# The opening's hand-written order changed by a few places in many entries, values loaded first, and late stores halved in place of late loads, in a fused linear-attention and PReLU-MLP kernel

## The chip, the cores and the metric

One core of one Trainium2 chip. The metric is the device time of one execution in microseconds (us); lower is better. The kernel before takes 220.07 us, the median of 3 runs (220.03 to 220.22).

## What is computed

Block-wise linear attention with a decay per head, and an MLP with a PReLU between its two matrices. q, k, v are (4 batches, 8 heads, 768 positions, 64), float32.

```python
for b in range(nb):                       # blocks of 64 positions
    intra = einsum('bhic,bhjc->bhij', qb, kb) * Dmask      # lam ** (i - j), causal
    intra = einsum('bhij,bhjd->bhid', intra, vb)
    inter = einsum('bhid,bhde->bhie', qb * lam_pow, kv_state)
    out[:, :, sl] = intra + inter
    kv_state = lam_block * kv_state + einsum('bhsd,bhse->bhde', kb * rev_pow, vb)
x = out.transpose(0, 2, 1, 3).reshape(3072, 512)
h = x @ w_in                              # 512 -> 2048
g = maximum(h, 0) + alpha * minimum(h, 0)
result = g @ w_out                        # 2048 -> 512
```

## The kernel before

**Tiling.** The 3072 positions are cut into 6 chunks c of 512: a third of the sequence (256 positions) of two batches. A chunk has four attention units, numbered n = 4c to 4c + 3: two batches (bi), two halves of the heads (hh, four heads each). On the kernel's own block size of 128 positions a unit has two blocks (a = 0, 1). The first four units, 0 to 3, are chunk 0; units 4 to 7 chunk 1, and so on.

**One unit.** `cast` (L267) copies its queries and keys to fp16; `turn` (L287) transposes them on TensorE, eight 128x128 transposes into the PSUM bank "tk", keys first, and `turned` (L300) copies the bank to qkT; from unit 8 on `turn_by_dma` (L305) does both as a DMA. `key_decayed` (L277) and `decayed` (L314) multiply keys and transposed queries by their decays. `cluster(old, new)` (L329) is TensorE's part: the scores s of the unit new, the output of the unit old from its masked scores sm and its states RD, and the state update kv of new, into the tile acc (or, with other=True, into banks 0 and 1, named h_acc). `masked` (L401) multiplies scores by the decay mask on VectorE. `state` (L418) makes the next state R from kv, on ScalarE where the state before is zero and on VectorE elsewhere; `spread` (L438) copies a state into the block-diagonal RD; `out_of` (L406) copies the unit's output to xT.

**The MLP.** `up(c, f, bi, slot)` (L453) makes 128 of the 2048 hidden features for a chunk, or for one batch of it (bi 0 or 1), in the PSUM bank slot; `below` (L466) is ScalarE's relu(-h), `gate` (L471) VectorE's combination of the two. `down` (L485) multiplies back, in four parts of four matmuls; `store` (L499) copies the result to SBUF on ScalarE and sends it out on ScalarE's DMA queue; `down_last` (L507) does both for the last chunk.

**Decays.** They depend on lam alone: `logs` takes logarithms, and `decay_mask`, `key_decay`, `query_decay`, `state_decay` (L201 to L224) exponentiate, all on ScalarE; `causal` (L206) clears the upper triangle of the masks on VectorE; `slopes` (L230) transposes alpha on TensorE into bank 0 and makes oma = 1 - alpha from it on VectorE.

**Loads.** `load` (L87) brings queries or keys as float32 on the SP queue, whole (512 KB) or a half of the heads (256 KB); `load16` (L100) brings queries or values as fp16 on POOL's queue, `load_win` and `load_wout` the weights likewise, a quarter each. `hold(x, c, bi)` (L83) writes one element of the tile that a load will fill, on VectorE: the load can't start before VectorE has reached that place in its order.

**The order.** The kernel turns the scheduler off. From L524 to the loop at L1097 each operation of the first three chunks is an entry in a list written out by hand; the engines run the entries in that order, each engine its own, and semaphores do the rest. A fixed PSUM bank is named by its slot. `fill(n, slot)` (L237) puts n matmuls of 128x128 on TensorE that nobody reads, into the bank of a slot (3 is the bank of the transposes). The loop from L1097 weaves the attention of the next chunk into the MLP of chunks 3 to 5, and loads two chunks ahead.

## Time and profile before

| | |
|---|---|
| median of 3 runs | 220.07 us |
| the profiled execution | 220.73 us |
| its span, first to last instruction | 218.6 us |
| TensorE (PE) busy | 207.1 us, 95% |
| VectorE (DVE) busy | 132.0 us, 60% |
| ScalarE (ACT) busy | 114.3 us, 52% |
| GpSimd (POOL) busy | 92.9 us, 43% |
| matmuls of fill | 132 of 2181 |
| mean granted TensorE clock | 0.999 |

The profile is of one execution. Times are from the first instruction of the span. A busy engine is one with an instruction in flight; TensorE's matmuls overlap, so that its busy time says that it was never idle, not that it ran at its peak. PEld is the weight load of TensorE, which overlaps with the matmuls; SP is the engine that only issues DMAs. A row of the timeline has the start in us, the length in us, engine, line, operation, what it writes and reads, the count, and in brackets how long the engine had been idle before it and what ended that. A row of the chain of waits has start, length and what the end of the kernel waited for then. A row of stretches has the window and its length, then for PE, PEld, DVE, ACT and POOL the busy time and the number of instructions, then clock, DMA share and GB/s. A row of DMA issues has what is loaded, the queue, the count, the size of one and the median us from issue to landing.

### The profile page before, as it was taken

Reading aid. Unit: us, or ns where it says so; the run is one execution under the profiler, and the core shown is the slowest. Engines: PE = TensorE matmul, PEld = TensorE weight load, DVE = VectorE, ACT = ScalarE, POOL = GpSimd, SP = SyncE. Lnnn points to the kernel's source line nnn. Section 1 sums busy time; section 2 is a strip of 40 time slices with the busy share of each in tenths; the row PEclk is TensorE's granted clock in tenths of the full one; section 3 lists DMA queues with packets and bytes.
Section 4 is the critical chain, followed back from the end, with each engine's and each line's share of the span. In section 5 each row is a group of like instructions: output and inputs, shape, how many; then the busy total and the mean of one; then the engine's idle time right before and its main releaser. Section 6 shows DMA issues by size and latency. Waiting matters only on the chain.

```text
span 218.6 us, 5366 instructions
## 1 busy us (share of the span) xinstructions
PE 207.1 (95%) x2181; PEld 112.5 (51%) x2181; DVE 132.0 (60%) x271; ACT 114.3 (52%) x225; POOL 92.9 (43%) x154
## 2 busy tenths in 40 slices
PE   4689799999999999999999999999999999999994
PEld 4577555564554554545445545554545444444442
DVE  2899488974688748778985646646645444444000
ACT  2996688741747534474746446445445444444120
POOL 8759996372546550736575374265231000000000
PEclk9999999999999999999999999999999999999999
DMA  3999999999999996499999441342211011110212
GB/s 105 231 190 221 191 212 219 214 210 204 312 229 197 305 212 209 60 143 163 250 236 121 97 96 33 66 96 59 40 51 48 1 51 48 48 45 3 99 48 97
DMA packets 62520, 29.85 MB, mean 137 GB/s; under 512 B 34192, under 2 KB 59552, under 8 KB 62496
## 3 DMA queue, kind: packets, MB, share of 16 engines
q1 hardware_dynamic: 38496, 15.01, 33.6%
q0 software_dynamic: 20368, 8.26, 30.6%
q10 hardware_dynamic: 3632, 6.24, 8.0%
q8 instruction: 17, 0.28, 0.5%
q14 instruction: 7, 0.06, 0.1%
HBM read 27.28 MB, written 6.29 MB: 154 GB/s over the span
## 4 chain that ended last, share of the span: by engine, by line
PE 78%; DMA 7%; ACT 6%; DVE 6%; issue 1%; ACTq 0%; DVEq 0%
PE h_ps L458 34%; PE o_ps L491 29%; PE o_ps L512 6%; DMA kraw<-in_k_dram 3%; PE s L363 3%; DMA qkT<-qk 2%; PE acc L375 2%; DMA lam_sb<-in_lam_dram 2%; PE acc L345 2%; DVE g L481 2%; ACT dmask L204 1%; ACT m L469 1%; DVE sm L404 1%; PE acc L392 1%; PE tp L294 1%
## 5 line engine op out<-in xcount | busy, mean ns | idle before, releaser
L481 DVE SCALAR_TENSOR_TENSOR g<-m,oma,h_ps 128x512 f16<-128x512 f32 (+1 forms) x104 | 72.0, 704 | 54.0 <-ACT m L469 53.6
L458 PE MATMUL h_ps<-xT,w_in_sb 128*128 128x512 f16 (+1 forms) x416 | 96.5, 363 | 0.5 <-DVE g L481 0.2
L469 ACT ACTIVATE m<-h_ps 128x512 f32<-128x512 f32 (+1 forms) x104 | 57.7, 563 | 60.0 <-PE h_ps L458 56.8
L491 PE MATMUL o_ps<-w_out_sb,g 128*128 128x512 f16 x320 | 79.9, 379 | 0.0
L458 PEld LDWEIGHTS <-w_in_sb 128*128 128x128 f16 x416 | 39.4, 98 | 42.6 <-issue 2.6
L491 PEld LDWEIGHTS <-g 128*128 128x128 f16 x320 | 30.5, 98 | 34.9
L255 POOL COPY RD<-R 64x128 f16<-64x128 f16 x54 | 16.2, 300 | 56.6 <-DVE R L429 54.7
L404 DVE TENSOR_TENSOR sm<-s,dmask 128x512 f16<-128x512 f32 x48 | 31.8, 683 | 3.3 <-PE s L363 3.2
L251 ACT ACTIVATE o_sb<-o_ps 128x512 f32<-128x512 f32 (+1 forms) x24 | 14.2, 592 | 22.4 <-PE o_ps L491 11.8
L282 POOL TENSOR_TENSOR kdec<-kraw,kdecay 128x512 f16<-128x512 f32 x21 | 22.2, 1061 | 1.9 <-DMA kraw<-in_k_dram 1.6
L319 POOL TENSOR_TENSOR qdT<-qkT,qdecay 128x512 f16<-128x512 f16 (+1 forms) x20 | 20.0, 1002 | 3.9 <-DMA qkT<-qk 3.1
L429 DVE SCALAR_TENSOR_TENSOR R<-R,rdecay,acc 128x64 f16<-128x64 f16 x60 | 13.9, 273 | 4.0 <-ACT xT L251 4.0
L251 ACT ACTIVATE xT<-acc 128x512 f16<-128x512 f32 x20 | 11.9, 596 | 7.9 <-PE acc L392 3.4
L241 PE MATMUL op_fill<-ident 128*128 128x128 f16 x132 | 10.5, 243 | 4.4 <-POOL ident masks.py:199 2.8
L512 PE MATMUL o_ps<-w_out_sb,g 128*128 128x512 f16 (+2 forms) x80 | 14.0, 336 | 0.0
L363 PE MATMUL s<-qkT 64*64 64x128 f16 x384 | 10.7, 222 | 1.4 <-DVE sm L404 0.8
L102 POOL DMA_DIRECT2D vh<-in_v_dram x13 | 11.7, 904 | 0.0
L241 PEld LDWEIGHTS <-ident 128*128 128x128 f16 x132 | 9.3, 111 | 4.6 <-POOL ident masks.py:199 2.8
L255 POOL CAST qk<-kraw 128x512 f16<-128x512 f32 x13 | 7.8, 610 | 8.1 <-DVE g L481 3.4
L512 PEld LDWEIGHTS <-g 128*128 128x128 f16 x80 | 7.2, 98 | 7.0
L363 PEld LDWEIGHTS <-qkT 64*64 64x64 f16 x384 | 6.5, 106 | 4.9 <-issue 1.4
L375 PE MATMUL acc<-sm,vh 64*64 64x128 f16 x352 | 8.8, 217 | 0.1
(69 smaller groups left out, 120.5 us busy)
## 6 DMA issues: line engine op xcount, KB each, us to landing
out_dram<-o_sb ACTq DMA_DIRECT2D x23, 256.0 KB, 2.2
kraw<-in_k_dram SPq DMA_DIRECT2D x12, 256.0 KB, 5.6
kraw<-in_k_dram SPq DMA_DIRECT2D x6, 512.0 KB, 8.3
qraw<-in_q_dram SPq DMA_DIRECT2D x6, 512.0 KB, 6.6
vh<-in_v_dram POOLq DMA_DIRECT2D x11, 256.0 KB, 6.8
w_in_sb<-in_moe_w_in_dram POOLq DMA_DIRECT2D x4, 512.0 KB, 8.9
w_out_sb<-in_moe_w_out_dram POOLq DMA_DIRECT2D x4, 512.0 KB, 15.4
qraw<-in_q_dram SPq DMA_DIRECT2D x5, 256.0 KB, 7.1
```

Source lines behind the costliest of these rows:

```text
L241: nc.tensor.matmul(t[:, 0:128], lhsT=ident, rhs=ident, start=True, stop=True)
L251: nc.scalar.activation(out, in_, AF.Copy)
L255: nc.gpsimd.tensor_copy(out=out, in_=in_)
L282: engine(eng).tensor_tensor(out=kdec, in0=kr, in1=d.unsqueeze(3).to_broadcast([128, 2, 4, D]), op=ALU.mult)
L319: engine(eng).tensor_tensor(out=qdT[:, :, :, p], in0=t["qkT"][:, 0, :, :, p], in1=qdecay[:, hh, :, :, p], op=ALU.mult,)
L363: nc.tensor.matmul(s[hl][ds(a * 64, 64), hp, 1 - e, :].rearrange("p (e j) -> p e j", e=2), lhsT=t["qkT"][p, 1, e, hp, ds(a * 64, 64)], rhs ...
L404: nc.vector.tensor_tensor(out=t["sm"][hl], in0=t["s"][hl], in1=mask_of(hl, units[n][2]), op=ALU.mult)
L458: nc.tensor.matmul(h_ps[:, 0:n] if bi is None else h_ps[:, 0:n].rearrange("p (e j) -> p e j", e=2), lhsT=w_in_sb[:, gi, ts(f, 128)], rhs=x ...
L469: nc.scalar.activation(m[:, 0:n], HP[c, f, bi][:, 0:n], AF.Relu, scale=-1.0)
L481: nc.vector.scalar_tensor_tensor(out=g, in0=mv, scalar=oma[:, f : f + 1], in1=hv, op0=ALU.mult, op1=ALU.add)
L491: nc.tensor.matmul(O[c, t], lhsT=G[c, f][:, t // 2, t % 2, :], rhs=w_out_sb[:, f, :], start=(f == 0), stop=(f == NF - 1),)
L512: nc.tensor.matmul(o_ps[:, 0:n], lhsT=G[c, f][:, t // 2, t % 2, :], rhs=w_out_sb[:, f, ds(c0, n)], start=(f == 0), stop=(f == NF - 1),)
```

## The change

- The list of the opening: nearly every entry up to turn(4) moves by a few places, many of the later ones by one or two. The first value load, load16("v", 0, 0, 1), becomes the first entry, ahead of the positions, and load16("v", 0, 0, 0) comes before identity. hold("k", 0, 1, 0) goes behind distances. slopes goes behind turn(1), turn(2) behind cluster(0, 1). hold("k", 1, 0) goes behind state(0, 1), hold("k", 1, 1) behind two gates. query_decay(3, 0) goes ahead of cast(4, "k").
- Engines: spread(0, 1), spread(4, 1), spread(9, 1) to ScalarE; cast(3, "q"), decayed(2), key_decayed(4), key_decayed(10), key_decayed(12), spread(11, 0) to VectorE; key_decayed(1) to POOL; spread(6, 1) stays there, two places later.
- fill: 165 matmuls in place of 132, in other places and banks.
- load("k", 4, bi) whole, the second half of the chunk first, in place of four halves; in the loop, for chunk 5, whole loads of keys and queries in place of halves.
- store: the results of chunk 4 and of the first two tiles of chunk 5 go out as two DMAs of 128x256 each in place of one of 128x512.

TensorE's order behind the opening is the same but for one place (up(1, 3, 1) goes behind down(1, 2, 2)).

```diff
@@ -501,8 +501,12 @@
         o_sb = o_pool.tile([128, DM], fp32, tag="osb", name="o_sb")
         copy_on("V" if last else "A", o_sb[:, 0:n], o_ps[:, 0:n])
         pb, b = c // 2, 2 * (c % 2) + t % 2
-        rows = out[ds(b * S + pb * W, W), ds(c0, n)].rearrange("(j e) d -> e j d", e=2)[t // 2]
-        (nc.sync if last else nc.scalar).dma_start(out=rows, in_=o_sb[:, 0:n])
+        w = n // 2 if (c, t) in HALVED else n
+        for x in range(0, n, w):
+            rows = out[ds(b * S + pb * W, W), ds(c0 + x, w)].rearrange("(j e) d -> e j d", e=2)[t // 2]
+            (nc.sync if last else nc.scalar).dma_start(out=rows, in_=o_sb[:, ds(x, w)])
+
+    HALVED = [(NC - 2, t) for t in range(4)] + [(NC - 1, t) for t in range(2)]
 
     def down_last(c, t, pieces):
         c0 = 0
@@ -521,132 +525,136 @@
 
 
 
+    load16("v", 0, 0, 1)
     positions()
-    warm_up()
-    load("q", 0, 0, 0)
-    identity()
-    load("k", 0, 0, 0)
-    hold("k", 0, 1, 0)
     load16("v", 0, 0, 0)
     distances()
+    load("q", 0, 0, 0)
+    warm_up()
+    hold("k", 0, 1, 0)
+    identity()
+    logs()
     load16("q", 0, 0, 1)
-    logs()
-    decay_mask(0)
+    load("k", 0, 0, 0)
+    cast(0, "k", "G")
+    load("k", 0, 1, 0)
+    query_decay(0, 0)
+    fill(38, 3)
     cast(0, "q", "A")
     key_decay()
-    query_decay(0, 0)
     decay_mask(1)
-    load16("v", 0, 0, 1)
-    cast(0, "k", "G")
     load_alpha()
-    fill(36, 2)
     turn(0)
+    load16("q", 0, 1)
     zeros()
     key_decayed(0, "V")
-    load16("q", 0, 1)
+    fill(6, 0)
     turned(0, "V")
+    decay_mask(0)
+    load_win(0)
+    load("k", 0, 0, 1)
+    fill(15, 2)
+    load16("v", 0, 1)
+    cluster(None, 0)
     decay_mask(3)
-    load("k", 0, 0, 1)
-    load16("v", 0, 1)
-    load_win(0)
+    query_decay(1, 1)
+    hold("k", 2, 0)
+    load16("v", 1, 0)
+    state(0, 0)
+    fill(6, 3)
     state_decay()
     decay_mask(2)
-    query_decay(1, 1)
-    fill(15, 2)
-    cluster(None, 0)
     causal(0)
-    load("k", 0, 1, 0)
-    state(0, 0)
-    hold("k", 2, 0)
+    spread(0, 1, "A", True)
+    fill(17)
+    cast(1, "k", "V")
+    fill(4, 2)
     cast(1, "q", "A")
-    cast(1, "k", "V")
-    fill(17)
-    spread(0, 1, "V", True)
-    load16("v", 1, 0)
     query_decay(0, 1)
+    turn(1)
     slopes(0)
-    fill(5, 2)
-    turn(1)
+    fill(5, 1)
+    key_decayed(1, "G")
+    load("k", 0, 1, 1)
+    query_decay(2, 1)
+    masked(0, 0)
     causal(1)
+    query_decay(3, 1)
+    fill(26, 2)
+    fill(14, 2)
+    masked(0, 1)
     cast(2, "q", "G")
-    masked(0, 0)
-    key_decayed(1, "V")
+    turned(1, "A")
+    cast(2, "k", "A")
     decayed(0, "G")
-    query_decay(3, 1)
-    turned(1, "A")
-    load("k", 0, 1, 1)
-    cast(2, "k", "A")
+    state(0, 1)
+    load16("q", 1, 0)
+    decayed(1, "G")
+    cluster(0, 1, True)
+    spread(1, 1, "A", True)
     hold("k", 1, 0)
-    masked(0, 1)
-    fill(26, 2)
+    cast(3, "k", "A")
     turn(2)
-    cluster(0, 1, True)
-    query_decay(2, 1)
-    state(0, 1)
-    cast(3, "k", "A")
-    decayed(1, "G")
-    load16("q", 1, 0)
+    state(1, 0)
+    masked(1, 0)
+    cast(3, "q", "V")
+    masked(1, 1)
+    turned(2, "A")
     load_win(1)
-    masked(1, 1)
-    cast(3, "q", "A")
-    masked(1, 0)
-    turned(2, "A")
+    spread(8, 0, "G")
+    fill(9, 2)
+    load16("q", 1, 1)
+    key_decayed(2, "V")
     key_decayed(3, "G")
-    spread(1, 1, "A", True)
-    state(1, 0)
-    spread(8, 0, "G")
+    cluster(1, None)
+    out_of(1, "A")
+    turn(3)
+    turned(3, "A")
+    cluster(None, 2)
+    fill(7, 0)
     out_of(0, "V")
-    fill(9, 2)
-    cluster(1, None)
-    key_decayed(2, "V")
-    decayed(2, "G")
-    load16("q", 1, 1)
-    turn(3)
-    out_of(1, "A")
-    cluster(None, 2)
+    up(0, 0, 0, 2)
+    decayed(3, "G")
+    query_decay(3, 0)
     load_win(2)
-    up(0, 0, 0, 2)
-    turned(3, "A")
     state(2, 0)
     spread(2, 1, "A", True)
+    decayed(2, "V")
     below(0, 0, 0)
+    load_win(3)
+    masked(2, 1)
     masked(2, 0)
-    load_win(3)
     state(1, 1)
-    masked(2, 1)
-    decayed(3, "G")
-    gate(0, 0, 0)
     fill(4, 0)
     cluster(2, 3, True)
+    gate(0, 0, 0)
     load("k", 1, 0)
     up(0, 2, 0, 2)
     cast(4, "k", "A")
-    key_decayed(4, "G")
-    query_decay(3, 0)
+    state(2, 1)
+    fill(14, 3)
+    key_decayed(4, "V")
+    state(3, 0)
     spread(3, 1, "A", True)
+    out_of(2, "A")
+    below(0, 2, 0)
+    load16("v", 1, 1)
+    up(0, 1, 0, 0)
     masked(3, 0)
-    state(3, 0)
-    out_of(2, "A")
-    state(2, 1)
-    fill(10, 3)
-    fill(10, 0)
-    up(0, 1, 0, 0)
     state(3, 1)
+    cast(4, "q", "V")
     masked(3, 1)
+    up(0, 3, 0, 1)
+    below(0, 3, 0)
+    below(0, 1, 0)
+    gate(0, 3, 0)
+    gate(0, 1, 0)
+    cluster(3, None)
+    out_of(3, "A")
     hold("k", 1, 1)
     load("k", 1, 1)
-    up(0, 3, 0, 1)
-    below(0, 3, 0)
-    cast(4, "q", "V")
-    cluster(3, None)
-    gate(0, 3, 0)
     turn(4)
-    out_of(3, "A")
-    below(0, 1, 0)
-    below(0, 2, 0)
-    gate(0, 1, 0)
     gate(0, 2, 0)
...
@@ -655,58 +663,58 @@
     cluster(None, 4)
     below(0, 2, 1)
     below(0, 6, None)
+    up(0, 0, 1, 0)
+    gate(0, 2, 1)
+    spread(10, 0, "G")
     below(0, 5, None)
     state(4, 0)
-    gate(0, 2, 1)
+    decayed(4, "G")
     load_wout(0)
-    key_decayed(5, "G")
+    load_wout(1)
     gate(0, 6, None)
-    load_wout(1)
-    up(0, 0, 1, 0)
     up(0, 4, None, 1)
-    spread(10, 0, "G")
     cast(5, "q", "G")
-    gate(0, 5, None)
     below(0, 0, 1)
     below(0, 4, None)
+    gate(0, 5, None)
     up(0, 8, None, 2)
-    decayed(4, "G")
     masked(4, 0)
+    load("k", 2, 0)
     turn(5)
-    load("k", 2, 0)
     state(4, 1)
+    key_decayed(5, "G")
+    below(0, 8, None)
     gate(0, 0, 1)
-    spread(4, 1, "G")
     cast(7, "q", "G")
     up(0, 3, 1, 0)
-    below(0, 8, None)
     spread(9, 0, "G")
+    spread(4, 1, "A")
     gate(0, 4, None)
     turned(5, "A")
     up(0, 7, None, 1)
     gate(0, 8, None)
     masked(4, 1)
     below(0, 3, 1)
+    up(0, 1, 1, 2)
...
@@ -860,14 +868,17 @@
     up(1, 15, None, 1)
     below(1, 13, None)
     cast(13, "k", "G")
+    below(1, 15, None)
     cluster(9, 10)
-    below(1, 15, None)
+    cast(12, "q", "G")
+    decayed(10, "G")
+    turn_by_dma(11)
+    key_decayed(12, "V")
     gate(1, 13, None)
     gate(1, 15, None)
     up(1, 12, None, 2)
     below(1, 9, None)
     gate(1, 9, None)
-    turn_by_dma(11)
     down(1, 0, 0, 1)
     state(10, 0)
     masked(10, 1)
@@ -875,24 +886,19 @@
     spread(10, 1, "A")
     up(1, 14, None, 0)
     key_decayed(11, "G")
-    cast(12, "q", "G")
     load16("v", 3, 0)
-    decayed(10, "G")
     below(1, 12, None)
     gate(1, 12, None)
     masked(10, 0)
     down(1, 0, 1)
-    key_decayed(12, "G")
     below(1, 14, None)
+    turn_by_dma(12)
     decayed(11, "G")
     gate(1, 14, None)
-    turn_by_dma(12)
     down(1, 0, 2)
     out_of(9, "A")
     cast(14, "k", "V")
     cluster(10, 11)
-    load("k", 4, 0, 0)
-    load("k", 4, 0, 1)
     cast(13, "q", "V")
     down(1, 2, 0, 0)
     key_decayed(15, "G")
@@ -902,12 +908,12 @@
     load("q", 4, 0)
     store(1, 0)
     down(1, 2, 1)
+    load("k", 4, 1)
+    down(1, 2, 2)
+    below(1, 2, 1)
+    load("k", 4, 0)
     state(11, 0)
     up(1, 3, 1, 1)
-    load("k", 4, 1, 0)
-    load("k", 4, 1, 1)
-    down(1, 2, 2)
-    below(1, 2, 1)
     load("q", 3, 1)
     spread(13, 0, "A")
     spread(11, 1, "G")
@@ -1097,9 +1103,8 @@
     for c in range(3, NC):
         if c + 2 < NC:
             for bi in range(2):
-                for x in ("k", "q"):
-                    load(x, c + 2, bi, 0)
-                    load(x, c + 2, bi, 1)
+                load("k", c + 2, bi)
+                load("q", c + 2, bi)
                 load16("v", c + 2, bi)
         att = attention_steps(c + 1) if c + 1 < NC else []
         moe = []
```

More of the change, by code (lines that the diff above doesn't have):

```diff
@@ L689 @@
     below(0, 3, 1)
+    up(0, 1, 1, 2)
+    gate(0, 3, 1)
+    cluster(4, 5)
+    hold("k", 3, 0)
+    load_wout(2)
+    up(0, 9, None, 0)
     load("q", 2, 0)
-    up(0, 1, 1, 2)
-    cluster(4, 5)
-    gate(0, 3, 1)
+    up(0, 11, None, 2)
+    below(0, 1, 1)
+    key_decayed(7, "G")
+    key_decayed(6, "G")
     decayed(5, "V")
-    hold("k", 3, 0)
-    below(0, 1, 1)
-    load_wout(2)
+    gate(0, 1, 1)
+    below(0, 7, None)
     cast(6, "q", "G")
-    up(0, 9, None, 0)
-    below(0, 7, None)
-    gate(0, 1, 1)
-    up(0, 11, None, 2)
     state(5, 0)
-    key_decayed(6, "G")
-    key_decayed(7, "G")
     spread(5, 1, "A")
+    gate(0, 7, None)
     masked(5, 1)
     out_of(4, "A")
-    gate(0, 7, None)
     below(0, 9, None)
@@ L718 @@
     state(5, 1)
+    below(0, 14, None)
+    cast(8, "k", "G")
     up(0, 10, None, 2)
@@ L721 @@
     cast(7, "k", "G")
-    below(0, 14, None)
     turn(6)
-    cast(8, "k", "G")
     gate(0, 14, None)
@@ L737 @@
     up(0, 13, None, 2)
+    gate(0, 15, None)
     below(1, 0, 0)
-    gate(0, 15, None)
-    spread(11, 0, "A")
     cluster(None, 6)
+    spread(11, 0, "V")
     down(0, 2, 0, 1)
+    decayed(6, "G")
+    gate(1, 0, 0)
     turn(7)
-    gate(1, 0, 0)
     below(0, 13, None)
@@ L767 @@
     down(0, 1, 1, 2)
+    masked(7, 0)
     down(0, 0, 0, 2)
-    load16("v", 2, 0)
-    spread(7, 1, "V")
     cast(9, "k", "V")
     down(0, 0, 1, 1)
+    decayed(7, "G")
     down(0, 2, 2, 2)
     down(0, 0, 2, 1)
+    query_decay(2, 0)
+    spread(7, 1, "V")
     down(0, 2, 3, 2)
@@ L822 @@
     below(1, 1, 1)
-    gate(1, 0, 1)
-    key_decayed(10, "G")
+    key_decayed(10, "V")
     cast(10, "q", "G")
     gate(1, 1, 1)
+    below(1, 6, None)
     decayed(9, "V")
     state(9, 0)
-    below(1, 6, None)
     gate(1, 6, None)
```

55 lines of the change are left out of this document (26 added, 29 removed).

## The prediction

> **What bounds it now.** I read the page first (shares, slices, chain), then the busy time by stretches, the waits of TensorE, and the chain and timeline of the first 27 us.
>
> ```profile
> PE 207.1 (95%) x2181; PEld 112.5 (51%) x2181; DVE 132.0 (60%) x271; ACT 114.3 (52%) x225; POOL 92.9 (43%) x154
> ...
> PE 78%; DMA 7%; ACT 6%; DVE 6%; issue 1%; ACTq 0%; DVEq 0%
> ```
> ```profile
> 20.00:24.75 4.75, 2.98 (x74) 2.47 (x75) 2.56 (x8) 2.68 (x9) 4.74 (x7) 1.00 1.40 186
> 24.75:45.00 20.25, 20.00 (x265) 12.03 (x265) 17.29 (x37) 15.00 (x33) 14.30 (x26) 1.00 1.25 214
> ```
> ```profile
> PE s L363 <- DVE sm L404: 0.4, 1, 0.4
> PE h_ps L458 <- DVE g L481: 0.2, 1, 0.2
> ```
> From 24.75 us on TensorE (second number of a stretch) is busy all the time; its named waits behind 25 us sum to 0.6 us. The order of its instructions stays the same behind the opening but for one swap. So the change is worth what it does to the moment at which TensorE becomes dense, plus what it adds to or takes from those 0.6 us. That moment hangs on one load:
>
> ```profile
> 13.85 1.14 DVE kdec L282
> ...
> 15.02 6.87 DMA kraw<-in_k_dram
> ...
> 22.00 0.63 ACT qk L251
> 22.63 0.29 ACT qdecay L224
> ...
> 23.98 0.73 PE op_fill L241 x10
> ...
> 24.75 1.03 PE h_ps L458 x8
> ...
> 26.25 0.55 PE tp L294 x8
> 26.80 0.35 PE h_ps L458
> ```
> The keys of chunk 1 (call it K10) may be loaded only when VectorE has reached hold("k",1,0), behind kdec, which ends at 14.99. They land at 21.89; ScalarE, which stands at cast(4,"k"), then copies the state and xT, and only then is bank 0 free for up(0,1).
>
> **The change, step by step.** Times are from the span's start; on ScalarE and VectorE an operation starts about 0.1 us before the one ahead has ended, so a step is a tenth shorter than a duration.
>
> ```profile
> 10.33 0.10 ACT rdecay L219
> 10.42 0.69 ACT dmask L204 x2
> ```
> ```profile
> 2.82 3.84 PE L241 MATMUL op_fill<-ident 128*128 128x128 f16 x36 [2.82 <-POOL ident masks.py:199]
> 2.96 0.94 POOL L102 DMA_DIRECT2D vh<-in_v_dram  x1
> ...
> 4.94 0.46 DVE L189 TENSOR_SCALAR lamc<-lam_sb 128x8 f32<-128x8 f32 x1 [2.36 <-DMA lam_sb<-in_lam_dram]
> ...
> 10.03 0.42 PE L363 MATMUL s<-qkT 64*64 64x128 f16 x16 [0.47 <-DVE qkT L253]
> ...
> 11.31 0.26 ACT L426 ACTIVATE R<-acc 128x128 f16<-128x128 f32 x1
> 11.46 0.62 ACT L251 ACTIVATE qk<-qh 128x512 f16<-128x512 f16 x1
> 11.60 0.59 DVE L253 CAST RD<-acc 64x128 f16<-64x128 f32 x2 [0.34 <-ACT R L426]
> ...
> 12.22 0.17 DVE L233 TENSOR_SCALAR oma<-at_ps 128x16 f32<-128x16 f32 x1
> 12.31 1.02 DVE L210 TENSOR_TENSOR dmask<-dmask,keep 128x384 f32<-128x384 f32 x2
> ...
> 12.76 1.02 ACT L251 ACTIVATE qkT<-tp 128x1024 f16<-128x1024 f16 x1
> ...
> 15.53 0.46 DVE L429 SCALAR_TENSOR_TENSOR R<-R,rdecay,acc 128x64 f16<-128x64 f16 x2
> ...
> 18.49 1.02 ACT L251 ACTIVATE qkT<-tp 128x1024 f16<-128x1024 f16 x1
> ...
> 19.56 0.55 ACT L251 ACTIVATE RD<-acc 64x128 f16<-64x128 f32 x2
> ```
> *Values first.* Two value loads now stand ahead of ident on POOL, 0.94 and about 0.75 us: ident comes 1.66 us later, the fills begin at 4.48 instead of 2.82. The positions come 0.94 later, hidden by the lam load, for which VectorE waits until 4.94. No engine has a wait on a value load in the profile, so values that land sooner release nobody. The 38 fills, if the clock opens again 3.5 us after the first (rows under the second rival), end at about 8.33; turn(0)'s eight transposes and 21 fills follow at 0.056 and end at 9.95, and the first cluster begins there instead of at 10.03: nothing lost.
>
> *ScalarE.* rdecay and dmask(2) (0.79) now stand behind the state copy R, which therefore starts at 10.52 instead of 11.31. But behind it come these 0.79, R's own step of 0.16 and the two RD copies that VectorE had (0.55, as at 19.56): cast(1,"q") at 12.02 instead of 11.46. Three qdecays of 0.29 follow, not two: qkT(1) at 13.43 instead of 12.76.
>
> *slopes behind turn(1).* turn(1) ends with the queries of that cast, at 12.91, and only then comes the transpose that oma waits for: oma at 13.15 instead of 12.22, +0.93, with sm, dmask and K10's release queued behind it on VectorE. From there to the release, kdec (1.14) is gone to POOL; the second sm (0.60) and both R (0.45) now stand ahead of it: 0.93 - 1.14 + 1.05 = +0.84. K10 is issued at 15.86 instead of 15.02.
>
> *turn(2) behind cluster(0,1).* The 45 fills end at 15.58, and that cluster starts its scores 0.04 later than before. turn(2) now follows it; ScalarE does RD, cast(3,"k") and the state copy first (0.57 + 0.52 + 0.16), so qkT(2), 1.02 long, ends at 18.77. turn(3) needs its bank, and takes 0.69 with the way to ScalarE: qkT(3) at 19.46 instead of 18.49, and with query_decay(3,0) ahead (0.29) RD(2) ends at 21.38 instead of 20.11. cluster(2,3) is 1.25 later. All of it lies in the 1.5 us that ScalarE waits for K10; what it costs if K10 comes early stands under the rivals.
>
> *After K10.* How long K10 takes now is the one unknown. The nearest rows:
> ```profile
> kraw<-in_k_dram SPq DMA_DIRECT2D x12, 256.0 KB, 5.6
> ```
> ```profile
> kraw<-in_k_dram SPq DMA_DIRECT2D x1, 512.0 KB, 9.4
> ```
> Half its size takes 5.6 us, the next whole key load 9.4. I take its own 6.87, since the same transfers are under way on POOL's queue: landing at 22.73. Then cast, state, RD and xT without qdecay's 0.29: up(0,1) at 24.50 instead of 24.75, with no fills behind the bank. This -0.25 is lost again:
>
> ```profile
> 23.55 0.66 ACT L251 ACTIVATE xT<-h_acc 128x256 f16<-128x256 f32 x2
> ...
> 24.24 0.47 DVE L429 SCALAR_TENSOR_TENSOR R<-R,rdecay,h_acc 128x64 f16<-128x64 f16 x2 [2.15 <-ACT xT L251]
> ...
> 24.63 0.68 DVE L404 TENSOR_TENSOR sm<-s,dmask 128x512 f16<-128x512 f32 x1
> ...
> 25.23 0.53 DVE L253 COPY qk<-qh 128x512 f16<-128x512 f16 x1
> ```
> VectorE's R still waits for the second xT, which ends at 24.73 (before 24.20). cast(4,"q") (0.53) now stands between it and the last sm, which ends at 26.28 instead of 25.31. cluster(3,None) waits for that sm and ends at 26.65 instead of 26.25; turn(4) takes its 0.45, without the 0.1 that stood behind it, and up(0,6) begins at 27.10 instead of 26.80: +0.30. In short, up(0,6) comes 4.37 us after the landing; the change breaks even if K10 lands within 6.57 us.
>
> *Further on.*
> ```profile
> 34.26 0.87 ACT L469 ACTIVATE m<-h_ps 128x256 f32<-128x256 f32 x2 [0.46 <-PE h_ps L458]
> ```
> RD of unit 4 comes to ScalarE (0.55) ahead of this 0.46 of waiting: 0 to 0.1, taken as 0. kdec(10) comes to VectorE (at most the 1.14 above) and RD(9) leaves it (0.59): 0 to 0.5, taken as 0, since TensorE waits for sm but once behind 25 us. K11, the next key load, is released behind two gates, about 1.8 us later; TensorE waited for nothing of it, so it has room that the trace doesn't measure: 0 to 1.8, taken as 0 (third rival). The whole loads for the halved ones, late in the kernel, have no waiter in the profile. The halved stores cost ScalarE's queue one more issue each:
>
> ```profile
> 174.53 0.34 ACTq L505 DMA_DIRECT2D out_dram<-o_sb  x1
> ...
> 176.49 0.60 ACT L469 ACTIVATE m<-h_ps 128x512 f32<-128x512 f32 x1 [0.93 <-PE h_ps L458]
> ```
> 0.34 us more stands against 0.93 us that ScalarE waits for TensorE right after; and the last store, which sets the end, is not halved.
>
> Sum: +0.30 us. The profiled execution took 220.73 us (span 218.6), 0.66 over the median; it would take 221.03, and the median 220.07 becomes 220.4.
>
> **Rivals.** *K10 comes quickly (faster).* If it lands in 5.6 us, ScalarE's next bound is cluster(2,3), whose end at about 22.4 gives xT at 23.55 and, by the same steps as above, up(0,6) at 26.17: -0.63, 219.4. It decides below 6.57 us. For it: K10 starts later, when earlier loads are further along. Against it: the load of queries ahead of w_in(1) on POOL is issued about 1 us sooner, and meets K10 on the same engines.
>
> *The clock opens later (slower).*
> ```profile
> 2.82 3.67 PE L241 MATMUL op_fill<-ident 128*128 128x128 f16 x33 [2.82 <-POOL ident masks.py:199]
> ```
> ```profile
> 10.51 1.12 PE L241 MATMUL op_fill<-ident 128*128 128x128 f16 x17
> ```
> 33 fills in 3.67 us are 107 ns each, 17 in 1.12 us are 56 ns: TensorE ran at half speed until about 6.3. There that time was idle anyway. Now 67 small matmuls (38, 8 and 21) stand between 4.48 and the first cluster; all at 107 ns they end at 11.65, 1.7 us late, and everything above waits for that cluster's state. Between 0 and 1.7 I take half: 0.85 + 0.30, 221.2. It decides as soon as the clock opens later than about 8 us.
> [...]
>
> *A stall later.* K11 lands late enough to stop turn(6), or a moved cast on POOL stops turn(7): some 0.5 us, 220.9.
>
> *The change does nothing there:* if oma did not hold VectorE, K10 would be issued as before and the sum would be -0.5; it is part of the first rival.
>
> **How the numbers follow.** A measurement of this kernel can tell about 0.2%, 0.44 us, from no change. The forecast's case (K10 in 6.5 to 7.6 us, 219.9 to 221.1) has 0.45: 0.28 of it within the bound, 0.17 above. K10 quick: 0.25, nearly all faster. The clock: 0.18, slower. The stall: 0.12, 0.05 of it within. Faster 0.24, same 0.34, slower 0.42. The range reaches from the quick case (219.4, a little less if the 0.6 us of waits shrink too) to the clock's upper part: 219.2 to 221.7. K10 at 9.4 us (+2.8) is left out with the rest.
>
> **What would show it.** In the profile after: the first fill near 4.5 us; oma near 13.2 and not 12.2; K10 issued near 15.9; ScalarE idle before cast(4,"k") until it lands; the last sm of unit 3 behind the copy of the queries; and TensorE dense from up(0,6) near 27.1. It would be wrong if K10's release is early, if the first cluster starts well behind 10 us, or if the time moves behind 45 us.

## The result, and the profile after

The changed kernel takes 228.16 us (median of 4 runs, 227.74 to 228.91); the kernel before, on the same chip, 220.14 (220.03 to 220.22). The ratio is 1.037, 95% interval 1.033 to 1.041: 8 us slower, where I had forecast 220.4. Ratios and intervals here and below leave out executions more than 1.5% above the fastest of the same kernel; medians are of all. The profiled execution took 228.91 us, its span 226.7.

Lines of the page after, in the order of those shown of before: the span, the busy shares, the granted clock in 40 slices, the chain by engine.

```profile
span 226.7 us, 5426 instructions
...
PE 209.8 (93%) x2214; PEld 115.1 (51%) x2214; DVE 136.9 (60%) x273; ACT 115.4 (51%) x228; POOL 89.9 (40%) x149
...
PEclk9999969999999969999999999999999999999999
...
PE 81%; DVE 5%; ACT 5%; DMA 5%; issue 2%; POOL 2%; ACTq 0%; POOLq 0%; DVEq 0%
```

TensorE's share fell from 95% to 93%, and in the row of the clock two slices show a 6, where all 40 of before show a 9. These two marks are the quickest way into the result: something happened near 30 us and something near 80 us. The waits of TensorE in the changed kernel (who waited for whom, total us, times, longest) name both:

```profile
PE op_fill L241 <- POOL ident masks.py:199: 5.1, 1, 5.1
PE h_ps L458 <- ACT xT L251: 3.8, 1, 3.8
PE h_ps L458 <- DVE g L481: 2.8, 2, 2.6
```

The first is the late start of the fills, as expected. The second and third are new: one gap of 3.8 us, one of 2.6. The stretches around them (start:end, length, busy time and count of PE, PEld, DVE, ACT, POOL, granted clock, DMA share, GB/s):

```profile
28.56:31.97 3.41, 3.08 (x31) 2.06 (x31) 2.03 (x6) 1.86 (x6) 0.33 (x2) 0.50 1.34 192
79.76:83.17 3.41, 2.71 (x7) 0.99 (x7) 3.32 (x8) 1.00 (x3) 0.00 (x0) 0.50 1.28 282
76.35:79.76 3.41, 1.50 (x55) 1.14 (x54) 3.41 (x2) 1.09 (x2) 2.84 (x3) 1.00 1.04 196
25.15:28.56 3.41, 0.00 (x0) 0.00 (x0) 1.29 (x2) 1.33 (x5) 1.33 (x2) 1.00 1.34 205
```

Rows one and two are the stretches at half speed (0.50), each 3.41 us long; rows three and four are the 3.41 us ahead of each. So in this execution each gap cost twice: the wait itself, and then up to 1.7 us, half of 3.41, because TensorE came back at half speed.

The same matmuls, matched in their order in both traces, run 5.3 us late from 28 us on, 4.9 late at 67, and 8.4 late from 106 us to the end. So the opening brought 5.3, the second gap some 4, and about 0.9 was gained on the way. The last store lands 2.03 us behind the last matmul (before 2.02): nothing at the end.

**The first gap.** The chain of waits of the changed kernel through its opening (start, length, what):

```profile
5.09 3.71 PE op_fill L241 x38
...
10.63 0.35 PE s L363 x16
...
11.16 0.28 ACT R L426
...
12.69 0.64 ACT qk L251
...
13.97 0.18 DVE oma L233
...
16.28 0.38 DVE R L429 x2
16.66 0.04 DVE kraw L85
...
16.71 10.40 DMA kraw<-in_k_dram
...
27.21 0.63 ACT qk L251
...
28.46 0.39 ACT xT L251
...
28.89 1.86 PE h_ps L458 x8
...
32.31 0.86 PE h_ps L458 x4
```

The keys of chunk 1 (K10) were issued at 16.71, 0.85 later than I had it, and took 10.40 us instead of 6.87. They landed at 27.11, and up(0,1) began at 28.89 (before 24.75), up(0,6) at 32.31 (26.80). What had moved past them is in GpSimd's instructions of the changed kernel:

```profile
16.16 0.82 POOL L110 DMA_DIRECT2D w_in_sb<-in_moe_w_in_dram  x1
16.98 0.66 POOL L255 COPY RD<-R 64x128 f16<-64x128 f16 x2
17.58 0.89 POOL L102 DMA_DIRECT2D qh<-in_q_dram  x1
```

w_in's second quarter, load_win(1), goes out 0.55 us ahead of K10; in the kernel before it followed K10 by 1.37 us (16.39 against 15.02):

```profile
16.39 0.77 POOL L110 DMA_DIRECT2D w_in_sb<-in_moe_w_in_dram  x1
```

Half of K10's 1024 packets had begun 3.1 us after its issue in the kernel before, and only 6.5 us after it here.

**The second gap.** The chain near 75 us, then VectorE's and GpSimd's instructions there:

```profile
74.24 1.45 DVE g L481 x2
75.69 4.05 DVE kdec L282
79.74 0.67 DVE g L481
...
80.45 1.86 PE h_ps L458 x4
```
```profile
75.61 4.14 DVE L282 TENSOR_TENSOR kdec<-kraw,kdecay 128x512 f16<-128x512 f32 x1
```
```profile
75.05 0.94 POOL L102 DMA_DIRECT2D vh<-in_v_dram  x1
76.02 1.17 POOL L319 TENSOR_TENSOR qdT<-qkT,qdecay 128x512 f16<-128x512 f16 x1
77.14 2.05 POOL L282 TENSOR_TENSOR kdec<-kraw,kdecay 128x512 f16<-128x512 f32 x2
```

One kdec on VectorE is 4.14 us long, and TensorE waits for the g behind it. It is key_decayed(12,"V"). Of VectorE's four other kdecs in this trace three took 0.69 us; the fourth, 1.05 us at 19.07, began while GpSimd's kdec was running and ended 0.55 us behind it. Here GpSimd's three products end at 77.14 + 2.05 = 79.19, and VectorE's kdec ends 0.56 us after that.

### The profile page after: what moved, and what is told of

Same layout as the page of the kernel before. It is cut to its first block, busy times and chain, and to the rows that moved or that the text cites. A ratio compares the mean times of both kernels' runs of the same rounds, so it can differ in the third digit from the quotient of the medians.

```text
span 226.7 us, 5426 instructions
## 1 busy us (share of the span) xinstructions
PE 209.8 (93%) x2214; PEld 115.1 (51%) x2214; DVE 136.9 (60%) x273; ACT 115.4 (51%) x228; POOL 89.9 (40%) x149
## 4 chain that ended last, share of the span: by engine, by line
PE 81%; DVE 5%; ACT 5%; DMA 5%; issue 2%; POOL 2%; ACTq 0%; POOLq 0%; DVEq 0%
PE h_ps L458 33%; PE o_ps L491 30%; PE o_ps L516 6%; DMA kraw<-in_k_dram 5%; PE s L363 3%; PE op_fill L241 2%; PE acc L375 2%; DVE kdec L282 2%; PE acc L345 2%; ACT m L469 1%; DVE g L481 1%; PE tp L294 1%; DVE sm L404 1%; PE acc L392 1%; ACT RD L251 1%
## 5 line engine op out<-in xcount | busy, mean ns | idle before, releaser
L458 PE MATMUL h_ps<-xT,w_in_sb 128*128 128x512 f16 (+1 forms) x416 | 97.5, 368 | 6.6 <-ACT xT L251 3.8
L255 POOL COPY RD<-R 64x128 f16<-64x128 f16 x52 | 15.3, 293 | 62.3 <-DVE R L429 60.8
L319 POOL TENSOR_TENSOR qdT<-qkT,qdecay 128x512 f16<-128x512 f16 (+1 forms) x19 | 19.4, 1019 | 15.0 <-ACT qkT L251 7.2
L282 POOL TENSOR_TENSOR kdec<-kraw,kdecay 128x512 f16<-128x512 f32 x19 | 20.0, 1058 | 0.3
L241 PE MATMUL op_fill<-ident 128*128 128x128 f16 x165 | 12.3, 235 | 5.2 <-POOL ident masks.py:199 5.1
L241 PEld LDWEIGHTS <-ident 128*128 128x128 f16 x165 | 11.0, 107 | 5.6 <-POOL ident masks.py:199 5.1
L255 POOL CAST qk<-kraw 128x512 f16<-128x512 f32 x13 | 8.3, 651 | 6.4 <-ACT m L469 3.8
L363 PE MATMUL s<-qkT 64*64 64x128 f16 x384 | 10.2, 222 | 0.5 <-DVE sm L404 0.4
L282 DVE TENSOR_TENSOR kdec<-kraw,kdecay 128x512 f16<-128x512 f32 x5 | 7.3, 1451 | 3.3 <-DMA kraw<-in_k_dram 3.2
```

The costliest lines, as they stand in the source:

```text
L241: nc.tensor.matmul(t[:, 0:128], lhsT=ident, rhs=ident, start=True, stop=True)
L255: nc.gpsimd.tensor_copy(out=out, in_=in_)
L282: engine(eng).tensor_tensor(out=kdec, in0=kr, in1=d.unsqueeze(3).to_broadcast([128, 2, 4, D]), op=ALU.mult)
L319: engine(eng).tensor_tensor(out=qdT[:, :, :, p], in0=t["qkT"][:, 0, :, :, p], in1=qdecay[:, hh, :, :, p], op=ALU.mult,)
L363: nc.tensor.matmul(s[hl][ds(a * 64, 64), hp, 1 - e, :].rearrange("p (e j) -> p e j", e=2), lhsT=t["qkT"][p, 1, e, hp, ds(a * 64, 64)], rhs ...
L458: nc.tensor.matmul(h_ps[:, 0:n] if bi is None else h_ps[:, 0:n].rearrange("p (e j) -> p e j", e=2), lhsT=w_in_sb[:, gi, ts(f, 128)], rhs=x ...
```

## The experiments

Two theories: **Q** (the queue), that K10 lands late because load_win(1) is now issued ahead of it; **P** (the products), that a VectorE product of two operands in memory is held as long as GpSimd's products follow one another. Their rivals (R and others) stand in the expectations. Sixteen runs were made, in four groups; the kernel before ran beside each group with medians of 219.83, 219.82, 219.99 and 219.85 us.

### e1: the decay of unit 12 back on GpSimd

```
-    key_decayed(12, "V")
...
     down(1, 0, 1)
+    key_decayed(12, "G")
```


> One line of the change undone: the decay of unit 12's keys goes back from VectorE to GpSimd, at its old place. Theory (the second gap is VectorE's kdec, held 4.1 us where others take 0.69): the gap of 2.6 us at 78 us goes, and with it the half-speed stretch of 3.41 us behind it, which costs 1.7: about 4 us less than the changed kernel, 224.2 us. Rival (the second gap comes from something that reached VectorE late, the halved loads or stores): another instruction is late there and the time stays within 1 us of 228.2.

226.05 us (1.029 of before, 1.023 to 1.035), 2.1 less than the changed kernel. The second gap is gone (TensorE's longest wait for g is 0.5 us), and each of its executions shows a mean clock of 0.992, one half-speed stretch, where two of the changed kernel's four had two (0.985). Those two took 228.91 and 228.03 us, the two with one stretch 228.28 and 227.74: the second stretch hardly shows in the times. K10 took 9.97 us: the first gap stayed. The gain is half of what I expected; in its trace the second gap's 4 us are gone, but K10 was issued 0.37 us later than in the changed kernel, and 0.5 us of wait for g stand near 42 us.

### e2: the same decay on VectorE, ahead of GpSimd's products

```
     masked(9, 0)
+    key_decayed(12, "V")
...
-    key_decayed(12, "V")
```


> The decay of unit 12's keys stays on VectorE, but stands right behind the masks of unit 9, where GpSimd has nothing to do (70.0 to 72.9 us in the changed kernel's trace); the keys have landed at 68.1. Theory (kdec and GpSimd's instructions exclude one another while both read two operands or one from memory): it takes 0.69 us, no gap at 78 us, about 224.2 us. Rival A (VectorE's kdec of chunk 3's keys is slow by its data or its wait): it takes some 4 us again, now at 71 us, and the time stays near 228. Rival B (a kdec on VectorE costs its 0.7 us wherever it stands): the gap shrinks but about 0.7 us stays.

kdec(12) ran at 72.67 in 0.68 us and left no gap behind:

```profile
72.67 0.68 DVE L282 TENSOR_TENSOR kdec<-kraw,kdecay 128x512 f16<-128x512 f32 x1
```

I had expected GpSimd idle there; it had casts, one ending at 72.75, the next from 72.69 on, but none of its products. 226.58 us (1.031, 1.027 to 1.035). Rivals A and B fall: neither the data nor VectorE as such makes it slow, only what GpSimd does at that moment. In the profiled execution (227.11 us) K10 took 11.52 us, and two half-speed stretches followed the first gap, which ate part of the gain.

### e3: w_in's second quarter behind the queries

```
-    load_win(1)
     spread(8, 0, "G")
     fill(9, 2)
     load16("q", 1, 1)
+    load_win(1)
```


> Only the issue of the second quarter of w_in is moved, behind the last load of queries on GpSimd's queue, some 1.7 us later. Theory Q (the keys of chunk 1 land late because their packets take turns with the large packets of w_in): they now meet the smaller packets of the queries first and land within 8 to 9 us of their issue, not 10.4; the first gap shrinks by 1.5 to 2.4 us: about 226.3. Theory R (landing depends on when they are issued and on the total in flight, not on which load they meet): 10 to 10.8 us again, 228 within 0.5. Against both stands that TensorE may then wait for w_in itself.

One moved issue brings back most of the loss, with both gaps: 222.33 us (1.013, 1.008 to 1.018). GpSimd's issues, then K10's answer by tile (issue near 17.0):

```profile
17.57 0.94 POOL L102 DMA_DIRECT2D qh<-in_q_dram  x1
18.51 0.76 POOL L110 DMA_DIRECT2D w_in_sb<-in_moe_w_in_dram  x1
```
```profile
DMA to landing us min/median/max: 6.0/6.0/6.0
```

K10, issued 0.27 us later than in the changed kernel, landed 4.1 us sooner, more than Q had promised. R falls. The first gap and both half-speed stretches are gone. The second gap is gone too, though its line was untouched: the kernel now ran so that VectorE came to kdec(12) at 72.33, ahead of GpSimd's qdT at 72.87, and it took 0.68.

### e4: the marker of K10 moved up

```
     masked(0, 0)
+    hold("k", 1, 0)
...
-    hold("k", 1, 0)
```


> Only the marker that releases the load of chunk 1's keys is moved up on VectorE, behind the first mask of unit 0: issued near 14.8 us instead of 16.7. Theory Q (the packets that it meets set its duration): the load now starts ahead of w_in's second quarter and meets the last values and the first queries; it lands in 7 to 8.5 us, near 22.5, up(0,1) comes at 24.3 and up(0,6) near 27; the first gap goes, and with it its half-speed stretch: about 5 us less, 223.2. Theory R (the duration is the same 10.4 us whenever it is issued): it lands at 25.2, 1.9 us sooner, the gap stays at 1.9 us; TensorE may keep its clock: 1.9 to 3.6 us less, 224.6 to 226.3.

222.57 us (1.012, 1.008 to 1.016). The other way round to the same order: K10 issued at 15.72, load_win(1) at 17.10, landing after 5.35 us. A load of queries was issued 0.49 us ahead of K10 here and did no harm. The second gap was left at 1.2 us, and its rows say more of P than any other:

```profile
72.14 2.73 DVE L282 TENSOR_TENSOR kdec<-kraw,kdecay 128x512 f16<-128x512 f32 x1
```
```profile
72.14 1.18 POOL L319 TENSOR_TENSOR qdT<-qkT,qdecay 128x512 f16<-128x512 f16 x1
73.27 1.05 POOL L282 TENSOR_TENSOR kdec<-kraw,kdecay 128x512 f16<-128x512 f32 x1
74.48 1.31 POOL L282 TENSOR_TENSOR kdec<-kraw,kdecay 128x512 f16<-128x512 f32 x1 [0.16 <-PE acc L392]
```

GpSimd had a pause of 0.16 us at 74.32. VectorE got in there and ended 0.56 later, at 74.87; now GpSimd's own kdec, which came second, is the long one (1.31 against 1.05).

The traces agree on kdec: it took 0.68 us where it came first (e3), and ended 0.55 or 0.56 us behind GpSimd's products where it came second; and VectorE did not get in between GpSimd's products where these follow without a pause: in the changed kernel it was held for three of them. Not every product on VectorE is held: sm, which reads the scores from PSUM, took 0.67 to 0.69 us in all 48 rows of the changed kernel, ten of them beside GpSimd's products, while dmask, with both operands in memory, took 1.36 us beside a kdec of GpSimd at 10.11 and 0.55 in its three other rows. What decides who is first stays open: in the changed kernel VectorE's row begins at 75.61, ahead of the first product at 76.02, while GpSimd issues a load, and it was held all the same.

### e5: on the kernel before, w_in's second quarter ahead of K10

```
+    load_win(1)
     decayed(1, "G")
     load16("q", 1, 0)
-    load_win(1)
```


> The other side of the queue theory, on the kernel before: only the issue of the second quarter of w_in goes up on GpSimd, to about 14.5 us, ahead of the queries and of the keys of chunk 1 (issued at 15.0 as before). Theory Q: the keys' 512-byte packets now take turns with w_in's large ones as in the changed kernel and take 8 to 10 us, not 6.9: landing at 23 to 25, 1 to 3 us of TensorE's time lost, more if the gap halves the clock: 221 to 225. Theory R (duration as in the kernel before, since nothing else in the opening moved): 220.1 within 0.5.

225.30 us (1.024, 1.020 to 1.027). One line, and two thirds of the loss, on a kernel whose opening is otherwise the old one. The chain and GpSimd's issue:

```profile
14.36 9.57 DMA kraw<-in_k_dram
```
```profile
13.72 0.81 POOL L110 DMA_DIRECT2D w_in_sb<-in_moe_w_in_dram  x1
```

The gap on TensorE was 4.2 us, and half speed followed at 26.65.

### e6: the old opening with the changed rest

The list of the kernel before stands up to the line ahead of this one, and from it on everything is the changed kernel's, loads and stores too:

```
     up(0, 6, None, 1)
```


> The list of the kernel before up to up(0,6), and from there the changed kernel's list, stores and loads. Theory (the opening's loss is the late keys, and of the rest only kdec of unit 12 costs, if it meets GpSimd's three instructions): 220.1 if VectorE comes to it while GpSimd is idle, up to 224 if it meets them as in the changed kernel; kdec(12) then shows more than 0.69 us. Rival (moved casts, whole loads or halved stores cost something of their own): over 220.6 without any long kdec.

218.46 us over 10 runs (218.19 to 219.28), 0.994 of before (0.992 to 0.996): a little faster than both kernels, and the best time that ran. kdec(12) met one of GpSimd's products here and took 1.44 us, without a gap on TensorE. So the moved casts, the whole loads and the halved stores together cost nothing that shows, and the kernel with the later list gains 0.6%. In the profiled execution the last matmul ends at 213.34 (before 215.34); 1.2 of these 2.0 us stand already at up(0,1), where K10 took 5.59 us instead of 6.87 from an opening that is the same. How much of the 1.4 us of the medians the later list gains by itself is not told apart; e1, e2, e3 and e9, which share that list and have no second gap, each gain 0.5 us against before behind 67 us in their traces.

### e7: idle matmuls in the first gap

```
-    fill(14, 3)
+    fill(80, 3)
```


> The changed kernel with 80 idle matmuls instead of 14 ahead of unit 2's second mask, about 3.7 us more of them: they lie in the first gap, which ends with the landing of the keys as before. [...] Rival (the half-speed stretch is a record only, and the loss lies in the wait alone): the time stays at 228.2 within 0.5.

225.38 us, the median of four; 1.024 of before (1.020 to 1.028) without the slowest. Three of the four executions had the clock at full speed throughout, and took 224.53, 224.58 and 226.18 us. The rival (a record only) falls by the changed kernel's own trace: the eight matmuls of up(0,1) take 1.86 us in the half-speed stretch at 28.89, and took 1.03 in the kernel before. How much of the time is the clock isn't told apart: more than the 1.7 us went, the second gap was smaller (1.34 us in the trace), and K10's landing in the three is not on record. The profiled execution (228.60 us) is the fourth: K10 took 12.39 us, and TensorE fell to half speed even so, after this stretch:

```profile
22.52:25.93 3.41, 1.35 (x55) 1.01 (x53) 1.49 (x6) 0.88 (x4) 2.76 (x4) 1.00 1.40 208
25.93:29.34 3.41, 3.41 (x30) 3.16 (x31) 0.00 (x0) 0.00 (x0) 0.00 (x0) 0.50 1.28 210
```

### e8: on the kernel before, K10 released sooner

```
+    hold("k", 1, 0)
     key_decayed(1, "V")
...
-    hold("k", 1, 0)
```


> The kernel before with one line moved: the marker that releases chunk 1's keys stands ahead of VectorE's kdec of unit 1, issue at 13.9 instead of 15.0. Theory Q (they meet the same small packets, ahead of w_in's second quarter): landing 0.8 to 1.1 us sooner, ScalarE's wait of 1.5 us before cast(4) shrinks by that, TensorE is dense 0.6 to 1.1 us sooner: 219.0 to 219.5. Theory R' (they now take turns with the first quarter of w_in and the values, which are still under way until 19.8): they land no sooner, 220.1.

219.94 us (1.000, 0.998 to 1.002): no change. In the trace VectorE was later for another reason (the product dmask, 1.84 us in place of 1.02), so that K10 was issued at 14.81, hardly sooner than before's 15.02; it landed after 5.17 us, 1.9 sooner, and the 1.55 us of wait behind it went, but 1.29 us of wait for a mask appeared ahead of cluster(0,1). It says little on R', since the issue hardly moved; the gain that Q had promised did not come.

### e9: three lines of the changed kernel mended

The edits of e1, e3 and e4 in one kernel:

```
     masked(0, 0)
+    hold("k", 1, 0)
...
     load16("q", 1, 1)
+    load_win(1)
...
     down(1, 0, 1)
+    key_decayed(12, "G")
```


> The changed kernel with three lines put elsewhere: w_in's second quarter behind the last queries, the marker of chunk 1's keys behind the first mask, the decay of unit 12's keys on GpSimd. Theory (these two collisions are the whole loss but for some 0.5 us that the rest of the list gains): no gap over 1 us, clock full from some 8 us on, 220 to 220.8 us. Rival (the new order of the opening has a price of its own, fills that begin 2.3 us later and a clock that opens later): 221.5 to 222.5, with TensorE dense 1 to 2 us later than in the kernel before.

221.91 us (1.008, 1.004 to 1.011), clock full in all ten executions. No gap is above 0.7 us. So the two collisions and the clock are some 6 of the 8 us, and the rival is right for the rest: the new opening has a price of its own. The first cluster begins at 10.88 (before 10.03):

```profile
9.62 1.33 PE L241 MATMUL op_fill<-ident 128*128 128x128 f16 x21
10.88 0.42 PE L363 MATMUL s<-qkT 64*64 64x128 f16 x16
```

and up(0,6) runs 0.9 us late with it. Matched with the kernel before, another 1.7 us are lost between 40 and 50 us, and 0.9 gained behind that. The chain of waits passes there through K11, the next key load:

```profile
28.10 9.40 DMA kraw<-in_k_dram
...
37.67 2.05 POOL kdec L282 x2
39.72 1.12 POOL qk L255 x2
```

K11 is issued 2.74 us later than in the kernel before (25.36) and lands at 37.50 (34.79); the load behind it lands at 44.66 (41.42). GpSimd takes each up within 0.2 us, and TensorE waits for GpSimd's casts (0.5 us) and, near 48 us, for the state's copy (0.64 us). So the later release of K11, my third rival, has a part in this price; no run separates it.

### e10: on the kernel before, the values first

```
+    load16("v", 0, 0, 1)
     positions()
+    load16("v", 0, 0, 0)
     warm_up()
     load("q", 0, 0, 0)
     identity()
...
-    load16("v", 0, 0, 0)
...
-    load16("v", 0, 0, 1)
```


> The kernel before, with only the two loads of values moved ahead of ident on GpSimd. My first step (nothing lost: the fills catch up, the first cluster still begins near 10.0): 219.8 within 0.4 of the kernel before. Rival (clock opens later, so that the fills run at half speed until behind 8 us and the first cluster moves by 0.5 to 1.7 us): 0.5 to 1.7 us slower.

220.13 us over 12 runs (1.000, 0.997 to 1.002). Nothing lost, as my first step had it. The fills begin at 5.08 and the first cluster at 10.06:

```profile
5.08 3.75 PE L241 MATMUL op_fill<-ident 128*128 128x128 f16 x36 [5.08 <-POOL ident masks.py:199]
...
9.12 1.00 PE L241 MATMUL op_fill<-ident 128*128 128x128 f16 x15
10.06 0.42 PE L363 MATMUL s<-qkT 64*64 64x128 f16 x16
```

Here 15 fills stand behind turn(0), where the changed kernel has 21: with them it starts at 10.56.

### e11: e6 with unit 12's decay on GpSimd

```
-    key_decayed(12, "V")
...
     down(1, 0, 1)
+    key_decayed(12, "G")
```


> The old opening with the changed rest (0.6% faster than the kernel before), and the decay of unit 12's keys back on GpSimd. There kdec(12) took 1.44 us on VectorE without a gap on TensorE behind it. Theory: the same 218.5 within 0.4, and the gain over the kernel before stands, so that it comes from other lines than this one. Rival (the gain hangs on taking this microsecond from GpSimd): 219.3 or more.

218.95 us over 12 runs (0.995, 0.991 to 0.998). The gain stands, so it does not hang on this line.

### e12 and e16: on the kernel before, the slopes behind turn(1)

```
-    slopes(0)
     fill(5, 2)
     turn(1)
+    slopes(0)
```


> The kernel before, with only the transposition of the slopes moved behind turn(1), so that oma, which VectorE's masks, kdec, and the release of chunk 1's keys stand behind, comes some 0.9 us later. By my third step the keys are issued 0.9 us later; if they take the same 6.87 us, ScalarE waits that much longer and the time is 0.5 to 0.9 us more: 220.4 to 220.7. Rival: VectorE catches up at its next wait (mask of unit 0, GpSimd's instructions), the keys are issued as before, and the time is the same within 0.4.

> The same kernel as with the slopes moved behind turn(1), once more. If its slower executions are the same collision: the keys issued behind w_in's second quarter or taking over 9 us, a gap of 3 us or more before cast(4), and the clock halved for 3.41 us behind it; 224.5 to 226. If something else slows it: keys in 7 us or less, and the loss at another place.

e12's six executions reach from 220.78 to 227.77 us, median 224.98; its profile is of the fastest, with K10 at 16.57, load_win(1) at 17.94, and 4.36 us to the landing. e16, the same kernel, took 224.56 (1.022, 1.007 to 1.036), and its profile is of the faster of two, 223.25 us:

```profile
15.44 8.70 DMA kraw<-in_k_dram
```
```profile
15.72 0.77 POOL L110 DMA_DIRECT2D w_in_sb<-in_moe_w_in_dram  x1
```

K10 has only 0.28 us on load_win(1) here, and takes 8.70. TensorE then waits 2.5 us for it. That is the collision again, in part; the half-speed stretch of this trace stands ahead of that wait, from 17.61 us on, not behind it as expected. Why the lead shrinks here and not in e12's fastest execution, where GpSimd's issue came later too (17.94), is open, and e12's five slower executions left no trace. The rival is wrong, and so was my price of 0.5 to 0.9.

### e13, e14, e15: what of the order matters

e13, on the kernel before, with the marker further down; e14, on the kernel before, with a load of queries ahead of K10; e15, on the changed kernel, with load_win(1) as four loads of 128 columns:

```
-    hold("k", 1, 0)
...
     masked(1, 1)
+    hold("k", 1, 0)
```
```
+    load16("q", 1, 1)
     decayed(1, "G")
...
-    load16("q", 1, 1)
```
```
-    load_win(1)
+    load_win(1, 4)
```


> The kernel before with the marker of chunk 1's keys moved down, behind unit 1's second mask: issued near 17.6 us, about 1.2 us behind w_in's second quarter, which is issued at 16.4 as before. Theory Q (who is issued first of these two decides): the keys take 9.5 to 12 us, landing 27 to 29.5, TensorE idle for 4 us or more, clock halved: 225 to 229. Theory R (6.9 us as in the kernel before, whenever issued): landing 24.5, 222.5 to 223.

> The kernel before with the last load of queries, not w_in, issued ahead of chunk 1's keys (near 13.7 us). If the kind of the load matters: keys in 4.5 to 7 us, 220 within 0.7. If anything ahead on GpSimd's queue does it: 8.5 us or more, 222 to 225.

> The changed kernel, w_in's second quarter at its place ahead of the keys, but in four loads of a quarter of the columns, so that its packets are a quarter as large (2,048 bytes before, 512 then, of the source). GpSimd spends 3.0 us on their issue in place of 0.8, so only the keys' time from issue to landing is read. If the size of the packets decides (packets of both queues take turns): 6 to 8 us. If the bytes ahead decide: 10 us or more.

e13: 226.62 us (1.031, 1.023 to 1.039). GpSimd's queue is the old one, only VectorE's marker moved:

```profile
16.41 9.31 DMA kraw<-in_k_dram
```

load_win(1) was issued 0.39 us ahead. Q holds, R falls: the order of the two counts, not who caused it. e14: 222.73 us (1.008, 1.003 to 1.013); K10 took 8.45 us in the profile, though load_win(1) followed it by 1.85. Three of its eight executions took 220.4 to 220.8, five 222.6 to 224.1. So a load of queries ahead (by 0.64 us) can do some of the harm, though in e4 one that was 0.49 us ahead did none: it isn't w_in alone, and the order isn't all of it. e15: 223.79 us (1.018, 1.010 to 1.027); K10 took 8.47 us, between the two expectations. Three of its four parts were issued behind K10, so packet size and bytes ahead are not told apart.

All traces in one table (lead: issue of load_win(1) minus issue of K10; then K10's time to landing, us):

| kernel | lead | landing | | kernel | lead | landing |
|---|---|---|---|---|---|---|
| e9 | 3.45 | 5.43 | | e8 | 1.29 | 5.17 |
| e10 | 1.54 | 5.44 | | e16 | 0.28 | 8.70 |
| e3 | 1.53 | 6.01 | | e13 | -0.39 | 9.31 |
| e6 | 1.43 | 5.59 | | changed | -0.55 | 10.40 |
| e4 | 1.38 | 5.35 | | e1, e2 | -0.55 | 9.97, 11.52 |
| before | 1.37 | 6.87 | | e7 | -0.55 | 12.39 |
| e11, e12 | 1.37 | 4.44, 4.36 | | e5 | -0.64 | 9.57 |
| e14 (queries ahead) | 1.85 | 8.45 | | e15 (first of four parts) | -0.55 | 8.47 |

But for e14 and e15 it takes 4.4 to 6.9 us with a lead of 1.3 us or more, and 9.3 to 12.4 behind load_win(1). At one and the same lead it still varies by some 2.5 us. The counts of packets begun show what the two queues did. In the changed kernel GpSimd's queue began 931 from 17.0 to 18.5 us, and K10, issued at 16.71, none; from 20.2 to 21.7 GpSimd's queue began 178, of some 1,000 bytes and 100 ns each, and K10 164, of 512 bytes and 40 ns: nearly one for one. In the kernel before, from 17.5 to 18.5, K10's queue began 457 and GpSimd's 177. That the packets take turns, as e3 expected of Q, is in line with the second count alone; no run here shows the turns themselves.

## Why the prediction was wrong, step by step

**Values first, 0.6 us short.** ident came at 5.05 instead of 4.43, since GpSimd issued its first load only at 1.24. e10 shows that the two loads cost nothing with the 51 fills that the kernel before has ahead of its first cluster; with the 59 of the changed kernel it starts 0.5 us late, where I had "nothing lost".

**ScalarE and oma, right in direction, 0.6 to 0.9 us short.** First cluster 10.56 (9.95 forecast), R 11.16 (10.52), cast(1,"q") 12.69 (12.02), oma 13.97 (13.15), K10's issue 16.71 (15.86). The error enters with ident, 0.6 us late, and runs through, growing to 0.85. It is not the late clock, to which I gave 0.18: in this trace the fills come 107 ns apart until 8.1 us, 3.0 us behind the first where I had 3.5, and 56 ns from there on.

**"I take its own 6.87, since the same transfers are under way on POOL's queue": this step failed, and brought most of the loss.** K10 took 10.40 us; e5, which moves nothing but load_win(1), lost 5.5 us; e13, which moves nothing but K10's marker (issued 1.39 us later), lost 6.8. The transfers were the same, their order wasn't. I had bounds of 5.6 and 9.4 and left the upper one out of the range with the rest; the measured 10.40 lies above both. I had the two lists that show the swap: K10's release moved behind unit 0's second mask and the state on VectorE, load_win(1) stayed where it was on GpSimd, and I had even forecast K10 0.84 later. 16.39 against 15.86 was already a lead of 0.5 instead of 1.37. I worked out when K10 was issued and never against what. e3, e4, e5 and e13 show it from all four sides.

**"kdec(10) comes to VectorE ...: 0 to 0.5, taken as 0": failed, 3.9 us in the trace.** By the medians e1 and e2, which take the collision out, are 2.1 and 1.6 us faster. kdec(10) itself took 0.69 us. I missed that key_decayed(12) moved to VectorE as well, and bounded both by 1.14, the longest row of before. That row was itself a collision: 13.85 to 14.99 beside GpSimd's qdT, which ended at 14.44, 0.55 sooner. Its cost alone is 0.69, and its bound is set by what GpSimd has in line. e2 shows it: the same instruction at another moment took 0.68 us.

**The return to half speed, missed.** I argued with the clock at the start and not with its return. The half speed behind the two gaps is 1.7 us each at most; e7's three executions without it are 2.0 to 3.6 us faster than the changed kernel's median, with a smaller second gap and whatever K10 did there included.

**Whole loads, halved stores, RD(4): right.** e6 has them all and is 0.6% faster than before; the forecast had no gain there.

**K11, "0 to 1.8, taken as 0": right in the changed kernel only.** There no wait of TensorE names it, behind a first gap that delays everything else too. e6 releases K11 at its old place and can't tell. Once the first gap is mended, in e9, K11 stands on the chain, and up to 1.7 us are lost behind it.

Of the rivals, "K10 quick" came true only where the lead was restored, and there it gave 222.3 and not 219.4, because the first cluster (10.88) and cluster(2,3) (23.15, before 20.17) are late by themselves, as e9 shows, and more is lost behind K11.

## What to carry to other kernels

Where two engines issue DMAs on queues of their own, work out the order of the issues across the queues, not each time by itself: here 2 us of lead on one load were worth 5 us. A duration read from one row is a price only after a look at what ran beside it; for products of two operands in memory on VectorE, look at GpSimd: kdec took 0.68 to 4.14 us here. And keep what is left when an edit is mixed: the rest of this change, without its opening, is the best version that ran.

## What the runs showed that I had not expected

- TensorE's clock fell to half for 3.41 us after stretches that were not idle: of the 3.41 us ahead 1.50 and 1.35 were busy (rows above), and 1.96, of mostly small matmuls, in e16, while 1.57 us in the same kernel were followed by full speed:

```profile
14.20:17.61 3.41, 1.96 (x62) 1.47 (x60) 3.25 (x8) 2.28 (x6) 3.39 (x6) 1.00 1.43 170
24.44:27.85 3.41, 1.57 (x18) 1.36 (x18) 1.29 (x5) 1.99 (x7) 3.39 (x5) 1.00 1.36 203
```

  The stretch from 17.61 us was at half speed, the one from 27.85 us was not. What decides is open; it is not the busy time alone. Nor is it the longest gap: one of 2.61 us stood ahead of half speed here, and in e16 1.45 us of idle time in all (3.41 less 1.96), while the wait of 2.5 us in the same kernel had full speed behind it.
- A product on VectorE took 3.45 us more than its 0.69 beside three of GpSimd's products in a row, whose rows leave no pause between them; a pause of 0.16 us (e4) let it in.
- The same load of 512 KB took 4.4 to 12.4 us, for the most part by what was issued ahead of it.
